# Reordering the opening transfers of a Fourier-mixing and ELU-MLP kernel: x first, then the filter in two halves, with the weight conversions spread anew

## The chip, the cores and the metric

The kernel runs on one core of one Trainium2 chip. The metric is device time in microseconds (us), the time of the slowest core, and here there is only one. Its engines are named as in the profile: PE is the matrix engine TensorE, PEld its weight loads, DVE is VectorE, ACT is ScalarE, POOL is GpSimd, SP is SyncE. "Landed" means that a transfer's completion was seen by whoever waited for it.

## The reference

Eight sequences of 3008 rows by 256 channels are filtered in the frequency domain, and every row then goes through an MLP with an ELU between its two matrices.

```python
batch, seq, dim = (8, 3008, 256)
X = np.fft.rfft(x, axis=1)
F = (filt_r + 1j * filt_i)[None, :, :]           # 1505 frequencies x 256
y = np.fft.irfft(X * F, n=x.shape[1], axis=1)
h = y.reshape(24064, 256) @ w_in                 # 256 x 2048
g = np.where(h > 0.0, h, np.exp(np.minimum(h, 0.0)) - 1.0)
out = g @ w_out                                  # 2048 x 256
```

## The kernel before

The transform of one sequence is split in stages, and between stages the data are turned round through DRAM. For the first sequence these stages run alone; those of the other seven run inside the MLP's work. The MLP is 192 "quads" of matmuls. The opening, which the change touches, has these parts:

- `x_load`: six chunks of x (two transfers of 256 KB each on the SyncE queue) and six tables `ta` (ScalarE queue). Only four chunk buffers exist.
- `a_unit`: four matmuls per chunk on TensorE, evicted by ScalarE (L168). `z_write` puts the result in DRAM, `z_read` brings it back in another order.
- `f_read_first`: the filter, 22 transfers on the GpSimd queue into one large buffer `ff`. Half `a = 0` lies on partitions 0 to 47, half `a = 1` on 64 to 110; `c` is 0 for the real part and 1 for the imaginary part.
- the filter loop: eight `b_unit`s. Each has four VectorE products with `ff` (L223 to L226), two GpSimd combinations, then inverse matmuls, and a write to DRAM (`y_write`).
- `w_fetch(k)`, `w_convert(k)`: 16 blocks of weights (512 KB each) are fetched on the GpSimd queue into three rotating buffers and turned from 64-bit to 32-bit numbers by VectorE and ScalarE. The odd blocks have four adds more.
- `y_read`, `n_unit`: the last stage (psn, L266), whose output the first quad needs.

```python
    def f_read_first(t):
        for c, src in enumerate((filt_r, filt_i)):
            for a in range(2):
                r = a * 64
                nc.gpsimd.dma_start(t[r:r + 24, :, c, :, :].rearrange("q g u d -> q g (u d)"),
                                    raw(src, 2 * a, [[64 * D, 24], [4 * D, NG], [1, 2 * D]]))
                for u in range(2):
                    g0 = 1 if a == u == 0 else 0
                    for r0, n in ((24, 16), (40, 7)):
                        nc.gpsimd.dma_start(t[r + r0:r + r0 + n, g0:NG, c, u, :], ...)   # cut: source rows
            nc.gpsimd.dma_start(t[24:48, 0, c, 0, :], raw(src, 32, [[64 * D, 24], [1, D]]))
# ... cut ...
            for k in range(2):
                w_fetch(k)
            for c in range(XBUFS):
                x_load(0, c, nc.scalar)
            nc.vector.memset(ff, 0.0)
            nc.gpsimd.tensor_copy(out=junk[0:1], in_=xs[0, 2][0:1, 0, 0:1])
            # ... cut: small tables ...
            w_fetch(2)
            f_read_first(ff)
            for c in range(NXC):
                a_unit(0, c)
                if c + XBUFS < NXC:
                    x_load(0, c + XBUFS, nc.scalar)
                z_write(0, c)
                w_convert(c)
                w_fetch(3 + c)
            z_read(0, 0)
            z_read(0, 1)
            for g in range(NG + 2):
                # ... cut: bi_unit(g - 2), b_unit(g), z_read(g + 2), y_write(g - 2) ...
                if g % 2 == 1:
                    k = 6 + g // 2
                    w_convert(k)
                    w_fetch(k + 3)
```

In the trace of this kernel ScalarE waits 21.16 us for a weight block while an eviction whose matmuls ended by 25 us stands behind it (the line is in the prediction); and GpSimd issues that block at 46.98 us, behind all 22 transfers of the filter (18.63 to 46.44 us).

Of the kernel before, what the change touches and what calls it, by code (L numbers as in the profile page):

```python
# [26 lines left out]
D = 256  # L27
# [5 lines left out]
NXC = H // XC  # L33
NG = K2 // 4
XBUFS = 4
# [60 lines left out]
def kernel(  # L96
# [9 lines left out]
    nc = tc.nc  # L106
# [37 lines left out]
    def raw(src, row, ap):  # L144
        return bass.AP(tensor=src.tensor, offset=src.offset + row * D, ap=ap)
# [15 lines left out]
    def a_unit(b, c):  # L161
        t = t1s[b, c] = t1p.tile([P, XC, D], FP32, tag="t1", name="t1")
        xt, w = xs.pop((b, c)), tas.pop((b, c))
        for r in (0, 2):
            ps = psM.tile([P, 2, D], FP32, tag="mx", name="psa")
            for u in range(2):
                nc.tensor.matmul(ps[:, u, :], w[:, r + u, :], xt[:, r + u, :], start=True, stop=True)  # L167
            nc.scalar.activation(out=t[:, r:r + 2, :], in_=ps, func=AXT.Copy)  # L168
# [19 lines left out]
        for a, r in enumerate((LO, HI)):  # L188
            nc.gpsimd.dma_start(t[r].rearrange("p c u d -> p (c u d)"), fd[g, a].rearrange("q c u d -> q (c u d)"))

    def f_read_first(t):


        for c, src in enumerate((filt_r, filt_i)):
            for a in range(2):
                r = a * 64
                nc.gpsimd.dma_start(t[r:r + 24, :, c, :, :].rearrange("q g u d -> q g (u d)"),
                                    raw(src, 2 * a, [[64 * D, 24], [4 * D, NG], [1, 2 * D]]))
                for u in range(2):
                    g0 = 1 if a == u == 0 else 0  # L200
                    for r0, n in ((24, 16), (40, 7)):
                        nc.gpsimd.dma_start(t[r + r0:r + r0 + n, g0:NG, c, u, :],
                                            raw(src, 64 * (r0 - 23) - 4 * g0 - 2 * a - u,
                                                [[64 * D, n], [-4 * D, NG - g0], [1, D]]))
            nc.gpsimd.dma_start(t[24:48, 0, c, 0, :], raw(src, 32, [[64 * D, 24], [1, D]]))



# [304 lines left out]
    with tc.manual_schedule():  # L513


        with tc.tile_pool(name="boot", bufs=1) as bp:
            ff = bp.tile([P, NG, 2, 2, D], FP32, name="ff")
            for k in range(2):
                w_fetch(k)
            for c in range(XBUFS):  # L520
                x_load(0, c, nc.scalar)
            nc.vector.memset(ff, 0.0)
            nc.gpsimd.tensor_copy(out=junk[0:1], in_=xs[0, 2][0:1, 0, 0:1])
            for t, d in ((gb, gb_d), (gr, gr_d), (gi, gi_d)):
                nc.gpsimd.dma_start(t, d)
            w_fetch(2)
            f_read_first(ff)
            for c in range(NXC):
                a_unit(0, c)
                if c + XBUFS < NXC:  # L530
                    x_load(0, c + XBUFS, nc.scalar)
                z_write(0, c)
                w_convert(c)
                w_fetch(3 + c)
            z_read(0, 0)
            z_read(0, 1)
            for g in range(NG + 2):
                if g >= 2:
                    bi_unit(0, g - 2)
                if g < NG:  # L540
                    b_unit(0, g, ff[:, g])
                    if g + 2 < NG:
                        z_read(0, g + 2)
                if g >= 2:
                    y_write(0, g - 2)
                if g % 2 == 1:
                    k = 6 + g // 2
                    w_convert(k)
                    w_fetch(k + 3)
        yp = pool("yp", 2)  # L550
        gp = pool("gp", 2)
        ep = pool("ep", 2)
        op = pool("op", 1)
        y_read(0, 0)
        w_convert(11)
        w_fetch(14)
        nc.scalar.dma_start(eye, id_d)
        n_unit(0, 0)
        x_load(1, 0)



        PER = 24
        plan = {}

        def at(quad, place, fn, *a):
            plan.setdefault((quad, place), []).append((fn, a))

        for c in range(1, XBUFS):
            at(c - 1, 0, x_load, 1, c)  # L570
        for k in range(12, 16):
            at((0, 0, 1, 2)[k - 12], 1, w_convert, k)
        at(0, 1, w_fetch, 15)
        at(3, 1, f_arrange)
        for f in fbufs:
            at(4, 1, nc.vector.memset, f, 0.0)
        for b in range(B):
            t = (b - 1) * PER
            if b > 0:
                for c, s in enumerate((0, 2, 3, 4, 6, 7)):  # L580
                    at(t + s, 0, a_unit, b, c)
                    nb, nxt = (b, c + XBUFS) if c + XBUFS < NXC else (b + 1, c + XBUFS - NXC)
                    if nb < B:
                        at(t + s, 0, x_load, nb, nxt)
                    at(t + s, 0, z_write, b, c)
                for g in range(NG + 2):
                    s = t + 9 + g
                    if g >= 2:
                        at(s, 1, bi_unit, b, g - 2)
                    if g < NG:  # L590
                        at(s, 1, b_unit, b, g)
                    if g >= 2:
                        at(s, 1, y_write, b, g - 2)
                for g in range(NG):
                    s = t + 7 + g
                    at(s, 1, f_read, b, g)
                    at(s, 1, z_read, b, g)
            for m, (s, place) in enumerate(((20, 0), (25, 1), (29, 1), (32, 0), (36, 0), (40, 0))):
                if b > 0 or m > 0:
                    at(t + s - (1 if m == 0 else 2), 0, y_read, b, m)  # L600
                    at(t + s, place, n_unit, b, m)
                at(t + PER + 4 * m + 5, 0, o_unit, b, m)

        items = [(b, m, q) for b in range(B) for m in range(6) for q in range(4)]
        for i in range(-PER, len(items) + 2):
            ups, up_tail = up_steps(*items[i]) if 0 <= i < len(items) else ((), None)
            downs, down_tail = down_steps(*items[i - 1]) if 1 <= i <= len(items) else ((), None)
            ups, downs = list(ups), list(downs)
            for k in "UDUDUDUUD":
                s = ups if k == "U" else downs  # L610
                if s:
                    s.pop(0)()
            for fn, a in plan.get((i, 0), ()):
                fn(*a)
            for k in "UDUDD":
                s = ups if k == "U" else downs
                if s:
                    s.pop(0)()
            if up_tail:
                up_tail()  # L620
            if down_tail:
                down_tail()
            for fn, a in plan.get((i, 1), ()):
                fn(*a)
# [32 lines left out]
```

## Time and profile before

| | before |
|---|---|
| median of 4 runs | 2763.99 us (2762.85 to 2765.96) |
| profiled span | 2761.7 us |
| last eviction of x (ACT L168) starts | 61.02 us |
| last z write landed / z read back | 68.3 / 73.7 us |
| filter: first issue / last landed | 18.6 / 53.4 us |
| second product step (DVE L224) starts | 75.40 us |
| last product of the loop ends | 115.55 us |
| psn starts | 131.14 us |

I use the second product step, not the first, as the mark where the loop runs: the first needs only the filter's real part, the second needs the imaginary part too. Before, the two are 0.6 us apart.

These are stretches of the kernel before, from the view that sums each engine's busy time in a window. Where stretches are shown, the columns are the window, its length, the busy time of each engine with its number of instructions, TensorE's granted clock as a share of full speed (PEclk), the share of the 16 DMA engines that was busy, and GB/s.

```profile
core 0: us, PE busy (x) PEld busy (x) DVE busy (x) ACT busy (x) POOL busy (x), PEclk, DMA share, GB/s
50.00:73.70 23.70, 2.86 (x11) 1.45 (x14) 13.86 (x29) 6.40 (x11) 3.91 (x7) 0.50 0.76 219
0.00:73.70 73.70, 19.04 (x59) 12.46 (x62) 33.12 (x55) 15.48 (x26) 22.61 (x44) 0.70 0.94 225
...
74.79:115.55 40.76, 28.16 (x115) 8.92 (x108) 36.59 (x58) 9.78 (x18) 21.18 (x20) 0.63 0.57 156
```

### The profile page before, as it was taken

To read this page: it belongs to the slowest core of one execution; us is meant where nothing else is said; L and a number is where in the kernel's file an instruction comes from. 1 tells how busy PE (TensorE), PEld (TensorE's weight loads), DVE (VectorE), ACT (ScalarE), POOL (GpSimd) and SP (SyncE) were. 2 spreads that over 40 slices of the span, in tenths; PEclk is the share of its full clock that TensorE was granted. 3 is DMA by queue.
4 is the path that set the end of the run, shared out by engine and by line. 5 is a ranking of instruction groups with operands and counts; after the bars stand their busy time and mean duration, and the time that the engine had idled before them with its cause. 6 is when DMAs were issued, how large, how long until landed. Compare 5 with 4: busy or idle time off the path is not lost.

```text
span 2761.7 us, 36465 instructions
## 1 busy us (share of the span) xinstructions
PE 2661.4 (96%) x13376; PEld 2281.0 (83%) x13376; DVE 2021.7 (73%) x3428; ACT 1331.3 (48%) x2281; POOL 268.4 (10%) x322
## 2 busy tenths in 40 slices
PE   2689999999999999999999999999999999999998
PEld 1288778987899878998789877898789987899887
DVE  4777877777776777767776787767877677777776
ACT  2254455544455444554455544454454544454544
POOL 3311210002000120001200021000210012000000
PEclk7599999999999999999999999999999999999999
DMA  9654421433114331242313332143321223110100
GB/s 227 174 136 119 106 56 30 115 90 99 43 47 117 76 91 37 70 115 71 79 50 87 87 88 68 37 106 94 97 61 39 72 69 94 37 39 19 25 22 16
DMA packets 141634, 214.51 MB, mean 78 GB/s; under 512 B 25268, under 2 KB 99142, under 8 KB 141456
## 3 DMA queue, kind: packets, MB, share of 16 engines
q1 hardware_dynamic: 122656, 173.60, 24.7%
q0 software_dynamic: 17792, 36.93, 5.4%
q8 instruction: 106, 1.74, 0.3%
q10 hardware_dynamic: 1008, 1.64, 0.2%
q14 instruction: 72, 0.59, 0.1%
HBM read 137.04 MB, written 78.12 MB: 78 GB/s over the span
## 4 chain that ended last, share of the span: by engine, by line
PE 86%; DVE 7%; ACT 3%; DMA 2%; issue 2%; POOL 0%; SPq 0%; DVEq 0%; ACTq 0%; POOLq 0%
PE po L385 37%; PE pha L312 11%; PE phc L312 11%; PE phd L312 11%; PE phb L312 5%; PE psa L167 3%; PE psn L266 2%; PE pva L211 2%; PE psr L211 2%; PE pso L424 2%; DVE g L317 1%; ACT e L323 1%; ACT e L324 1%; DVE c L403 1%; DVE g L328 1%
## 5 line engine op out<-in xcount | busy, mean ns | idle before, releaser
L385 PE MATMUL po<-g,wo 128*128 128x256 f32 (+1 forms) x5376 | 1324.2, 375 | 0.0
L385 PEld LDWEIGHTS po<-g,wo 128*128 128x128 f32 x5376 | 1021.5, 190 | 116.2
L323 ACT ACTIVATE e<-g 128x512 f32<-128x512 f32 (+1 forms) x576 | 357.6, 621 | 599.5 <-DVE g L317 599.3
L324 ACT ACTIVATE e<-e 128x512 f32<-128x512 f32 (+1 forms) x768 | 477.6, 622 | 24.4
L312 PE MATMUL pha<-y,wi 128*128 128x256 f32 (+1 forms) x1536 | 396.3, 380 | 8.7 <-ACT g L332 8.6
L317 DVE TENSOR_TENSOR g<-phc,g 128x512 f32<-128x512 f32 (+1 forms) x384 | 259.5, 676 | 194.9 <-PE phc L312 194.8
L328 DVE SCALAR_TENSOR_TENSOR g<-e,g 128x512 f32<-128x512 f32 (+1 forms) x576 | 387.4, 673 | 11.6 <-ACT e L324 11.1
L323 ACT ACTIVATE e<-pha 128x512 f32<-128x512 f32 (+1 forms) x192 | 113.0, 588 | 531.1 <-PE pha L312 531.1
L312 PEld LDWEIGHTS pha<-y,wi 128*128 128x128 f32 x1536 | 285.2, 190 | 93.1 <-ACT t L238 34.1
L317 DVE TENSOR_TENSOR g<-phd,g 128x512 f32<-128x512 f32 (+1 forms) x384 | 261.0, 680 | 87.0 <-PE phd L312 66.0
L328 DVE SCALAR_TENSOR_TENSOR g<-e,pha 128x512 f32<-128x512 f32 (+1 forms) x192 | 129.4, 674 | 257.8 <-ACT e L324 257.8
L227 POOL TENSOR_TENSOR sr<-sr,sp 128x512 f32<-128x512 f32 x64 | 81.1, 1268 | 1304.4 <-DVE sp L225 1304.4
L312 PE MATMUL phc<-ys,wi 128*128 128x256 f32 (+1 forms) x768 | 195.5, 377 | 2.6 <-DVE si L224 2.6
L312 PE MATMUL phd<-y,wi 128*128 128x256 f32 (+1 forms) x768 | 195.4, 377 | 1.3
L312 PE MATMUL phb<-ys,wi 128*128 128x256 f32 (+1 forms) x768 | 193.8, 375 | 0.4 <-DVE ys L290 0.4
L312 PE MATMUL phc<-y,wi 128*128 128x256 f32 (+1 forms) x768 | 194.0, 375 | 0.0
L312 PE MATMUL phd<-ys,wi 128*128 128x256 f32 (+1 forms) x768 | 193.7, 375 | 0.0
L312 PEld LDWEIGHTS phc<-ys,wi 128*128 128x128 f32 x768 | 145.3, 191 | 23.7 <-issue 7.8
L312 PEld LDWEIGHTS phd<-y,wi 128*128 128x128 f32 x768 | 145.3, 191 | 22.5 <-PE phc L312 6.5
L332 ACT ACTIVATE g<-pha 128x512 f32<-128x512 f32 (+1 forms) x192 | 112.7, 587 | 105.3 <-PE pha L312 105.1
L312 PEld LDWEIGHTS phb<-ys,wi 128*128 128x128 f32 x768 | 145.8, 190 | 17.2 <-PE pha L312 0.7
L312 PEld LDWEIGHTS phd<-ys,wi 128*128 128x128 f32 x768 | 145.8, 190 | 16.5
(98 smaller groups left out, 2781.1 us busy)
## 6 DMA issues: line engine op xcount, KB each, us to landing
z<-t SPq DMA_DIRECT2D x192, 128.0 KB, 3.8
t<-z SPq DMA_DIRECT2D x128, 192.0 KB, 3.7
yd<-t SPq DMA_DIRECT2D x128, 192.0 KB, 2.8
t<-yd SPq DMA_DIRECT2D x192, 128.0 KB, 4.1
xc<-in_x_dram SPq DMA_DIRECT2D x88, 256.0 KB, 4.6
out_dram<-o SPq DMA_DIRECT2D x176, 128.0 KB, 2.4
f<-fd POOLq DMA_DIRECT2D x112, 192.0 KB, 3.6
tn<-tn_t SPq DMA_DIRECT2D x48, 256.0 KB, 4.2
```

The lines of the kernel that those rows point to most:

```text
L167: nc.tensor.matmul(ps[:, u, :], w[:, r + u, :], xt[:, r + u, :], start=True, stop=True)
L211: nc.tensor.matmul(ps[:, u:u + w, :], table[k, v, :], rhs[k, u:u + w, :], start=True, stop=True)
L227: nc.gpsimd.tensor_tensor(out=sr, in0=sr, in1=p, op=ALU.subtract)
L266: nc.tensor.matmul(ps[:, ts(q, P)], t[:, i - 4 * m, ds(dh * P, P)], w[:, i - 4 * m, :], start=True, stop=True)
L312: nc.tensor.matmul(banks[key][:, a, 0:h], w_in[q][:, COMBO[n], a, :], y[n], start=start and a == 0, stop=True, skip_group_check=True)
L317: nc.vector.tensor_tensor(out=g[o], in0=i0, in1=i1, op=ALU.add)
L323: nc.scalar.activation(out=e, in_=src, func=AXT.Relu, scale=-1.0)
L324: nc.scalar.activation(out=e, in_=e, func=AXT.Exp, scale=-1.0)
L328: nc.vector.scalar_tensor_tensor(out=g[n], in0=es[n], scalar=1.0, in1=src, op0=ALU.subtract, op1=ALU.max)
L332: nc.scalar.activation(out=g["t1"], in_=mm(1, "a", True), func=AXT.Copy)
L385: nc.tensor.matmul(po[i][:, u, 0:h], w_out[q][:, COMBO[n], a, :], g[n][:, a, :], start=q == 0 and a == 0 and n in (1, 3, 6, 4), stop=True, ...
L424: nc.tensor.transpose(ps[0:w, u, ts(dh, P)], c[dh][:, ds((2 * a + u) * P, w)], eye)
```

## The change

Its intent: nothing that the first products don't need should stand before x, so that x, z and the z read are done early; the filter follows, half by half; conversions fill the waits, so that fewer are left for the MLP.

```diff
-    def f_read_first(t):
+    def f_read_first(t, a):
+        r = a * 64
         for c, src in enumerate((filt_r, filt_i)):
-            for a in range(2):
-                r = a * 64
             ... (one main and four mirrored transfers per c, as before)
-            nc.gpsimd.dma_start(t[24:48, 0, c, 0, :], ...)
+            if a == 0:
+                nc.gpsimd.dma_start(t[24:48, 0, c, 0, :], ...)
...
+        CONVERTS = {0: 6, 1: 7, 3: 8, 5: 9, 7: 10, 8: 11}
+            def after(c):
+                nc.gpsimd.tensor_copy(out=junk[0:1], in_=xs[0, c][0:1, 0, 0:1])
-            nc.vector.memset(ff, 0.0)
-            nc.gpsimd.tensor_copy(out=junk[0:1], in_=xs[0, 2][0:1, 0, 0:1])
+            nc.gpsimd.memset(ff, 0.0)
+            w_convert(0)
...
             w_fetch(2)
-            f_read_first(ff)
+            w_fetch(3)
             for c in range(NXC):
+                if c + XBUFS < NXC + 2 and c >= 2:
+                    x_load(0, c + XBUFS - 2, nc.scalar)
+                if c == NXC - 1:
+                    after(NXC - 1)
                 a_unit(0, c)
-                if c + XBUFS < NXC:
-                    x_load(0, c + XBUFS, nc.scalar)
                 z_write(0, c)
-                w_convert(c)
-                w_fetch(3 + c)
+                if c == 1:
+                    w_convert(1)
+            f_read_first(ff, 0)
+            w_convert(2)
+            w_fetch(4)
+            w_fetch(5)
+            f_read_first(ff, 1)
             z_read(0, 0)
             z_read(0, 1)
+            for k in range(3, 6):
+                w_convert(k)
+                w_fetch(k + 3)
...
-                if g % 2 == 1:
-                    k = 6 + g // 2
+                if g in CONVERTS:
+                    k = CONVERTS[g]
                     w_convert(k)
                     w_fetch(k + 3)
...
-        w_convert(11)
-        w_fetch(14)
+        for k in (12, 13):
+            w_convert(k)
+            if k == 12:
+                w_fetch(15)
...
-        for k in range(12, 16):
-            at((0, 0, 1, 2)[k - 12], 1, w_convert, k)
-        at(0, 1, w_fetch, 15)
+        for k in (14, 15):
+            at(k - 14, 1, w_convert, k)
```

More of the change, by code (lines that the diff above doesn't have):

```diff
@@ L189, in f_read @@
             nc.gpsimd.dma_start(t[r].rearrange("p c u d -> p (c u d)"), fd[g, a].rearrange("q c u d -> q (c u d)"))
-    def f_read_first(t):
+    def f_read_first(t, a):
+        r = a * 64
         for c, src in enumerate((filt_r, filt_i)):
-            for a in range(2):
-                r = a * 64
-                nc.gpsimd.dma_start(t[r:r + 24, :, c, :, :].rearrange("q g u d -> q g (u d)"),
-                                    raw(src, 2 * a, [[64 * D, 24], [4 * D, NG], [1, 2 * D]]))
-                for u in range(2):
-                    g0 = 1 if a == u == 0 else 0
-                    for r0, n in ((24, 16), (40, 7)):
-                        nc.gpsimd.dma_start(t[r + r0:r + r0 + n, g0:NG, c, u, :],
-                                            raw(src, 64 * (r0 - 23) - 4 * g0 - 2 * a - u,
-                                                [[64 * D, n], [-4 * D, NG - g0], [1, D]]))
-            nc.gpsimd.dma_start(t[24:48, 0, c, 0, :], raw(src, 32, [[64 * D, 24], [1, D]]))
+            nc.gpsimd.dma_start(t[r:r + 24, :, c, :, :].rearrange("q g u d -> q g (u d)"),
+                                raw(src, 2 * a, [[64 * D, 24], [4 * D, NG], [1, 2 * D]]))
+            for u in range(2):
+                g0 = 1 if a == u == 0 else 0
+                for r0, n in ((24, 16), (40, 7)):
+                    nc.gpsimd.dma_start(t[r + r0:r + r0 + n, g0:NG, c, u, :],
+                                        raw(src, 64 * (r0 - 23) - 4 * g0 - 2 * a - u,
+                                            [[64 * D, n], [-4 * D, NG - g0], [1, D]]))
+            if a == 0:
+                nc.gpsimd.dma_start(t[24:48, 0, c, 0, :], raw(src, 32, [[64 * D, 24], [1, D]]))
     def tile_mm(ps, table, k, rhs, special):
```

## The prediction

> **What bounds the kernel now.** I read the page first, then the chain of waits over the first 180 us, then the same stretch in order of time and by stage. On the page TensorE is 96% busy and the chain that ended last is 86% TensorE, so outside the opening almost nothing is to be had; the kernel is 192 FFN quads after a start. The change touches only that start: the first 185 us or so of 2761.7. The stretches of it:
>
> ```profile
> core 0: us, PE busy (x) PEld busy (x) DVE busy (x) ACT busy (x) POOL busy (x), PEclk, DMA share, GB/s
> 20.00:30.00 10.00, 3.79 (x16) 2.71 (x16) 5.13 (x12) 1.20 (x2) 3.65 (x7) 0.98 1.10 253
> 30.00:40.00 10.00, 0.00 (x0) 0.00 (x0) 1.45 (x3) 1.09 (x2) 4.37 (x8) 0.50 1.06 201
> ...
> 50.00:60.00 10.00, 0.00 (x0) 0.00 (x0) 5.10 (x11) 2.82 (x5) 2.14 (x4) 0.50 0.79 228
> ...
> 90.00:100.00 10.00, 6.25 (x30) 2.10 (x23) 9.37 (x16) 3.28 (x6) 4.25 (x5) 0.67 0.60 179
> ```
>
> Until 50 us the transfers are the limit (share over 1, 200 to 250 GB/s) and every compute engine is idle half the time or more. From 75 to 115 us (the filter loop, eight units) VectorE is the limit: 9.4 of 10 us here, of which the weight conversions are nearly half. The chain says which transfers:
>
> ```profile
> 20.04 13.04 DMA ff<-in_filt_r_dram
> 33.08 0.28 issue
> 33.36 0.55 POOL ff L205
> 33.90 11.16 DMA ff<-in_filt_i_dram
> ...
> 47.58 6.99 DMA f<-in_moe_w_out_dram
> ...
> 63.43 4.87 DMA z<-t
> 68.36 4.28 DMA t<-z
> ...
> 120.92 3.78 DMA yd<-t
> ...
> 126.00 5.00 DMA t<-yd
> ```
>
> First the filter (all its 22 transfers go out on the GpSimd queue between 18.6 and 47.0 us), then the weight block of conversion 3, queued behind the filter, only then the last z write and read back. Why a weight block can hold x is seen in the order of time on ScalarE:
>
> ```profile
> 32.43 1.09 ACT L168 ACTIVATE t<-psa 128x512 f32<-128x512 f32 x2 [3.48 <-DMA z<-t]
> ...
> 54.67 0.67 ACT L471 ACTIVATE wl<-f 128x512 f32<-128x512 uint32 x1 [21.16 <-DMA f<-in_moe_w_out_dram]
> ...
> 55.77 1.06 ACT L168 ACTIVATE t<-psa 128x512 f32<-128x512 f32 x2
> ...
> 61.02 1.07 ACT L168 ACTIVATE t<-psa 128x512 f32<-128x512 f32 x2
> ```
>
> ScalarE works in program order. Conversion 3 stands ahead of the eviction of x chunk 4, so that eviction waits 21.16 us for a weight block, though its matmuls ended by 25 us; chunk 5's eviction comes at 61.02 for the same reason. The first filter product (VectorE) starts at 74.79, the last product ends at 115.55, the FFN's first matmuls (psn) at 131.14. One more place, behind the first FFN quad:
>
> ```profile
> 153.31 1.86 PE L312 MATMUL pha<-y,wi 128*128 128x224 f32 x4 [7.05 <-ACT g L332]
> ```
>
> Conversions 12 and 13 run together there (VectorE 148.09 to 157.1), TensorE is idle 7.05 us, and its granted clock falls to a half for some 10 us.
>
> [...] z writes issued from 20 to 40 us, beside the filter, took about 16 us to land, against 3.8 us in the median of the whole kernel. So holding the filter back really speeds x and z; it doesn't remove bytes. [...] the first two conversion steps take 0.43 us alone, 0.88 and 1.49 us when the GpSimd add of a filter unit runs. [...] VectorE's clearing of ff takes 6.88 us, so I estimate GpSimd's at 6 to 9 us. No long GpSimd clear is in the trace to test that.
>
> **The change, part by part.**
>
> *Clearing ff* moves to GpSimd: VectorE is free 6.88 us sooner, GpSimd sits in it from about 2.6 to 10 us. Before, GpSimd then waited until 15.77 for x chunk 2, so the small tables and weight block 2 go out some 5 us earlier than they did, and block 3 soon after. Some 1.2 MB now meets x chunks 2 and 3 (at 230 GB/s up to 5 us of sharing, perhaps 2 us of delay).
>
> *x first.* Chunks 4 and 5 now come after z writes 0 and 1 in the SyncE queue, but nothing of the filter goes out until chunk 5 has landed. In the trace z writes 0 went out at 15.9; I put z 1 at 19 to 20, chunk 4 out at about 23 and chunk 5 at about 28, landed at 34 to 35 (7 us, the landing time of x issued from 10 to 20 us). No weight stands ahead of the evictions that could be late (conversions 0 and 1 only), so the last eviction is at about 37 instead of 62.1. That is 25 us off the first chain, but it is not the gain.
>
> *Filter.* Half 0 (12 transfers, 1.5 MB) goes out from 35, beside the z writes 3 to 5; at 0.6 us an issue and with waits for earlier landings about 10 us. Then blocks 4 and 5 (the latter waits for conversion 2, whose ScalarE part stands behind the last eviction: done at about 41), then half 1 from about 46. Blocks and half are 2.5 MB, at 230 to 260 GB/s 10 to 11 us: landed at about 57 to 58. The z read back is earlier: last z landed at about 46, read by 51. Cross-check by bytes: x 3.1, ta 1.6, z 3.1, filter 3.0, six weight blocks 3.0, z read 0.8, tables 0.2: 14.8 MB, at 250 GB/s 59 us.
>
> *Conversions 3 to 5* now stand before the first filter unit. From this trace a conversion is 3.74 us of VectorE alone (60.03 to 63.77), 5.46 with the four combining adds (54.66 to 60.12). Conversion 5 can start when block 5 has landed and 4 is done, about 54, and ends at about 60. So first filter product at about 61 (transfers and VectorE nearly tie) instead of 74.79: **14 us gained**, give or take 6.
>
> *Filter loop.* Before, conversions 6, 7 and 8 stood ahead of the last product; now 6, 7, 8 and 9. Beside GpSimd one with adds takes 6.98 us (90.24 to 97.22). VectorE was busy 36.6 of the 40.8 us, so about 1.5 us of idle absorbs some: **5.5 us lost**. Then 10 and 11 instead of 9 and 10 in the ScalarE order before the last eviction: **about 1 lost**. Conversions 12 and 13 fill the 10 us in which yd is written and read (VectorE needs 10 plus 11, 12, 13 there, about 20 us from the last product; psn's eviction came 17.7 after it): at most 1 to 2 us over, **1 lost**.
>
> *FFN.* One conversion (14) after quad 0, one (15, with adds) after quad 1, none after quad 2, in place of two, one, one. After quad 0 5.4 us of VectorE and ScalarE waiting go, and the gap shrinks to about 2[...]: 10 groups at half clock from 153.31 on cost up to 3 us. After quad 1 1.7 us more VectorE work. **7 gained.**
>
> Sum: 14 - 5.5 - 1 - 1 + 7 = 13.5, and I round to 14: 2764 - 14 = **2750 us**.
>
> **Rivals.** (a) *Half 1 of the filter takes the place of the weight wait, and later than I think*: it is queued behind block 5 and so behind all of A's evictions; if its transfers take 25 us as two halves did before (18.6 to 54), the first product is at 70 and the gain is 5: 2759. For it: z writes and weight blocks still share. Against: the old filter shared with x, ta and z together. (b) *The loop takes nothing and the transfers run well*: first product at 56, conversion 9 mostly in idle time, clock kept in the FFN: gain 25, 2739. For it: weights issued after 50 us landed in 4.5 us. Against: VectorE idle in the loop is only 4.2 us. (c) *x comes later*: chunks 4 and 5 behind two z writes on SyncE, and ScalarE stalls in its own issue of ta 4 and 5 ahead of evictions; if chunk 5 lands at 45, all that follows is 10 later: 2760. (d) *No gain at all*, the bytes being the same: the DMA share of 0.79 from 50 to 70 speaks against it: there was room, and nobody to ask for it.
>
> **Range and chances.** The sum's worst likely combination is 0 to 3 gained, the best 27: 2737 to 2763. 2% is 55 us, nearly the whole stretch before the first filter product, and no part offers it; a loss of 55 would take a new stall as long as the whole filter.
>
> **What would show it.** The last x eviction at 35 to 40 us with no wait on a weight; filter transfers none before about 33; the first product of the filter at 58 to 64, ended by conversion 5 or the filter; last product 45 to 47 us after the first (40.8 now); no 7 us gap after quad 0 and no fall of the clock there. I am wrong if chunk 5 lands after 42, if half 1 lands after 65, or if the loop stretches by over 9 us.

## The result, and the profile after

Ratios in this document are the mean time of one kernel's fast runs over that of the other's of the same rounds, so they are not quite the ratio of the medians quoted beside them; a 95% interval stands in brackets.

| | runs | median us | lowest to highest | ratio to before |
|---|---|---|---|---|
| before | 4 | 2763.99 | 2762.85 to 2765.96 | |
| after | 4 | 2767.73 | 2762.17 to 2770.96 | 1.0011 [0.9993, 1.0028] |

By the 2% mark that is the same time. It is not the 2750 us that I predicted, and it lies outside my range of 2737 to 2763. The four runs of the kernel after are spread over 8.8 us, those of before over 3.1 us; that spread will matter. The profile fell on the slowest of the four, 2770.96 us, so the pieces below are those of a slow execution.

| us | before | after | difference |
|---|---|---|---|
| last eviction of x starts | 61.02 | 36.68 | -24.3 |
| x chunk 5 landed | 41.1 | 34.5 | -6.6 |
| last z write landed | 68.3 | 51.0 | -17.3 |
| z read back | 73.7 | 67.0 | -6.7 |
| filter, last landed | 53.4 | 76.0 | +22.6 |
| second product step | 75.40 | 76.00 | +0.60 |
| last product ends | 115.55 | 125.44 | +9.89 |
| psn starts | 131.14 | 144.21 | +13.07 |
| span | 2761.7 | 2769.2 | +7.5 |

The differences of the last four rows, taken piece by piece, are +0.60 up to the second step, +9.29 in the loop (40.15 to 49.44 us), +3.18 from the loop to psn (15.59 to 18.77), and -5.57 from psn to the end (2630.56 to 2624.99). They add up to +7.5.

The chain of waits of the kernel after (start, length, what):

```profile
34.35 7.46 DMA ff<-in_filt_r_dram
...
42.10 9.09 DMA ff<-in_filt_i_dram
...
51.47 15.36 DMA ff<-in_filt_r_dram
...
68.02 10.52 DMA f<-in_moe_w_out_dram
```

Compare it with the chain of before: x, z and the weight blocks among them have gone, and the chain runs through nothing but the filter from 34 to 67 us, then through weight block 6, fetched on the same queue behind it. That x really comes first is one line on ScalarE, the last eviction:

```profile
36.68 0.60 ACT L168 ACTIVATE t<-psa 128x512 f32<-128x512 f32 x1 [0.22 <-PE psa L167]
```

In brackets is the wait: 0.22 us for the matmul, and no weight block. The GpSimd queue of the kernel after shows where the second half stood:

```profile
49.59 0.68 POOL L196 DMA_DIRECT2D ff<-in_filt_r_dram  x1 [3.11 <-DMA ff<-in_filt_i_dram]
...
65.16 0.57 POOL L201 DMA_DIRECT2D ff<-in_filt_i_dram  x1 [1.32 <-DMA ff<-in_filt_r_dram]
```

The first transfer of half 1 went out at 49.59 us, the last at 65.16, although an issue costs only some 0.6 us (0.68 and 0.57 in these two lines): ahead of seven of the ten issues GpSimd waited 0.30 to 3.69 us, 13.4 us together, for earlier transfers of the filter or a weight block to land. So slow transfers delayed the issue of the next. And the transfers were slow:

```profile
core 0: us, PE busy (x) PEld busy (x) DVE busy (x) ACT busy (x) POOL busy (x), PEclk, DMA share, GB/s
45.35:75.97 30.62, 7.83 (x20) 2.13 (x20) 9.51 (x19) 2.40 (x4) 9.79 (x17) 0.50 1.04 168
...
50.00:60.00 10.00, 1.93 (x4) 0.73 (x4) 4.37 (x9) 1.92 (x4) 4.26 (x8) 0.50 1.04 182
60.00:70.00 10.00, 5.90 (x16) 1.40 (x16) 5.14 (x10) 0.49 (x1) 2.92 (x6) 0.50 1.07 137
...
76.00:125.44 49.44, 31.75 (x108) 8.63 (x108) 42.67 (x68) 11.71 (x21) 21.80 (x21) 0.50 0.52 145
...
0.00:76.00 76.00, 25.05 (x68) 14.23 (x68) 27.61 (x56) 15.29 (x25) 29.49 (x45) 0.74 0.99 215
```

The first line runs from the issue of weight block 4 to the landing of half 1: 30.62 us at 168 GB/s are 5.1 MB, of which blocks 4 and 5 and half 1 are 2.6 MB. The rest is z: the last z writes (landed by 51.0) and the z reads of the first four units (issued from 46.2 on), with the end of half 0 and, from 67.4 on, the first of weight blocks 6 to 8. In the two windows from 50 to 70 us the DMA share is over 1, so the engines were taken all the time, yet they moved 182 and then only 137 GB/s. Over the whole opening it is 215 GB/s for 76 us, 16.3 MB: about what before moved by 73.7 us. The fourth line is the loop: VectorE is busy for 42.67 us in place of 35.98 from the second step on. Where those went is in its order of time:

```profile
76.00 0.69 DVE L224 TENSOR_TENSOR si<-psr,ff 128x512 f32<-128x512 f32 x1 [6.51 <-DMA ff<-in_filt_i_dram]
...
111.24 1.12 DVE L470 TENSOR_SCALAR wm<-f 128x512 uint32<-128x512 uint32 x1
...
118.38 0.68 DVE L223 TENSOR_TENSOR sr<-psr,ff 128x512 f32<-128x512 f32 x1
...
122.96 0.69 DVE L223 TENSOR_TENSOR sr<-psr,ff 128x512 f32<-128x512 f32 x1 [2.11 <-PE psi L211]
```

The first line is the second product step: it waits for the imaginary part of the filter. The second and third are the beginning and the end of conversion 9, which stood behind the last product before: 118.38 - 111.24 = 7.14 us. The fourth is a wait of 2.11 us for TensorE. Before, the loop had two such waits, of 1.04 and 2.11 us; after it has three, of 1.04, 2.11 and 2.11. So 7.14 + 2.11 = 9.25, nearly the 9.29 us. (Summed over the whole loop, VectorE's busy time grew by 6.69 us and its idle time by 2.60, in which a wait of 0.76 us for weight block 6 is new too.) TensorE's granted clock in the loop is 0.50 in place of 0.63, which goes with that third wait; what lowers it I have not tested.

What the change did win, behind the first quad of the MLP, on TensorE:

```profile
163.10 1.86 PE L312 MATMUL pha<-y,wi 128*128 128x224 f32 x4 [3.40 <-ACT g L332]
```

The gap is 3.40 us where it was 7.05.

### The profile page after: what moved, and what is told of

Same layout as the page of the kernel before. It is cut to its first block, busy times and chain, and to the rows that moved or that the text cites. A ratio compares the mean times of both kernels' runs of the same rounds, so it can differ in the third digit from the quotient of the medians.

```text
span 2769.2 us, 36476 instructions
## 1 busy us (share of the span) xinstructions
PE 2668.7 (96%) x13376; PEld 2280.8 (82%) x13376; DVE 2018.0 (73%) x3427; ACT 1332.5 (48%) x2281; POOL 275.9 (10%) x323
## 4 chain that ended last, share of the span: by engine, by line
PE 86%; DVE 7%; ACT 3%; issue 2%; DMA 2%; POOL 0%; DVEq 0%; SPq 0%; ACTq 0%; POOLq 0%
PE po L385 37%; PE pha L312 11%; PE phc L312 11%; PE phd L312 11%; PE phb L312 5%; PE psa L167 3%; PE psn L266 2%; PE pva L211 2%; PE psr L211 2%; PE pso L424 2%; DVE g L317 1%; ACT e L323 1%; ACT e L324 1%; DMA ff<-in_filt_r_dram 1%; DVE c L403 1%
## 5 line engine op out<-in xcount | busy, mean ns | idle before, releaser
L312 PEld LDWEIGHTS phc<-ys,wi 128*128 128x128 f32 x768 | 144.8, 190 | 23.7 <-issue 7.8
```

The costliest lines, as they stand in the source:

```text
L312: nc.tensor.matmul(banks[key][:, a, 0:h], w_in[q][:, COMBO[n], a, :], y[n], start=start and a == 0, stop=True, skip_group_check=True)
```

## The experiments

All kernels of one call ran on one chip and share the runs of the kernel before. "Opening" is the time of the second product step in the profiled run. Where an expectation names a theory by a letter, H is the theory that the order by half is at fault (a half lies on one side of the partitions), and O that holding the filter behind x is.

| run | median us (runs) | before, same call | ratio | opening us | span us |
|---|---|---|---|---|---|
| after_again | 2768.70 (5) | 2762.88 | 1.0019 [1.0005, 1.0033] | 75.86 | 2767.1 |
| by_part | 2764.85 (5) | 2762.88 | 1.0008 [0.9995, 1.0020] | 70.76 | 2763.1 |
| blocks_last | 2773.54 (4) | 2762.88 | 1.0038 [1.0024, 1.0052] | 81.88 | 2773.8 |
| before_halves | 2763.95 (4) | 2762.88 | 1.0005 [0.9991, 1.0019] | 75.06 | 2761.9 |
| source_straight (wrong result) | 2762.06 (1) | 2762.71 | | 69.69 | 2760.3 |
| both_sides (wrong result) | 2764.83 (1) | 2762.71 | | 68.90 | 2763.1 |
| one_side | 2769.84 (1) | 2762.71 | | 75.23 | 2768.1 |
| old_converts | 2762.25 (5) | 2762.71 | 0.9998 [0.9984, 1.0011] | 69.72 | 2757.9 |
| alternate | 2762.05 (5) | 2762.57 | 0.9995 [0.9982, 1.0007] | 69.36 | 2760.3 |
| filter_early | 2770.25 (5) | 2762.57 | 1.0026 [1.0013, 1.0040] | 76.96 | 2770.0 |
| filter_early_old | 2767.40 (5) | 2762.57 | 1.0019 [1.0007, 1.0032] | 78.26 | 2768.1 |
| alone | 2919.61 (1) | 2762.57 | | | 2917.8 |
| alternate_old | 2758.31 (5) | 2762.69 | 0.9984 [0.9970, 0.9997] | 68.66 | 2757.5 |
| two_queues | 2760.85 (5) | 2762.69 | 0.9995 [0.9982, 1.0007] | 73.57 | 2759.6 |

### after_again: the kernel after, once more

No edit; it shows how far the result repeats.

> The changed kernel once more, as the yardstick of this call. All theories: 2762 to 2771 us, the filter's second half issued from about 49.6 us and landed at about 76, first filter product complete in its four steps only then. If the second half lands here by 65, the 26 us of the first profile were an accident of that execution and the case is another.

Measured: 2768.70 us, ratio 1.0019 [1.0005, 1.0033]. The second half went out at 50.2 and landed at 75.8 us. The result repeats, and the kernel after is slower by about 0.2%, a difference that is real and far below the 2% mark.

### by_part: the filter by component instead of by half

Both halves of the real part are issued first, then, at the place of the second half, both halves of the imaginary part.

```diff
-    def f_read_first(t, a):
-        r = a * 64
-        for c, src in enumerate((filt_r, filt_i)):
+    def f_read_first(t, c):
+        src = (filt_r, filt_i)[c]
+        for a in range(2):
+            r = a * 64
```

> The changed kernel, with the 22 filter transfers split between the two places by component (all real ones first, 11, then all imaginary ones, 11), not by half of the partitions; bytes, weights and places in the queue are otherwise the same. Theory H (a lone half is slow: all its transfers go to partitions 64 to 111 and read one half of each 4 KB): the second batch takes about 13 us, lands at about 62 to 64, the first filter product is at about 65 in place of 75 and the time falls by about 10, to 2757. Theory W (the second batch is late because two weight blocks stand before it and its last issues wait for their landing): as the changed kernel, landed at about 74 to 76, 2766. Theory B (the same bytes, so the same end): as W.

Measured: the second batch went out at 48.6 and landed at 70.7 us, 22.1 us where the half took 26.4, and the opening is 5.2 us earlier than in the kernel after. The time is 2764.85. In the mean of five runs each, it is 3.2 us faster than after_again (2765.13 against 2768.36). So the order of the same transfers matters, by some 3 us; the 5 us of the two profiles are less sure, because an opening of one order varies as much (see old_converts). And 70.7 is far from the 58 that I had predicted: the order by half is not the whole cause.

### blocks_last: weight blocks 4 and 5 behind the second half

```diff
             w_convert(2)
+            f_read_first(ff, 1)
             w_fetch(4)
             w_fetch(5)
-            f_read_first(ff, 1)
```

> The changed kernel with weight blocks 4 and 5 fetched after the filter's second half. Theory H: the half still goes slowly once alone, 18 to 20 us, but starts about 4 us earlier and shares less: landed at about 65 to 68; blocks 4 and 5 land at about 70, conversion 5 ends at about 76, so the first product is no earlier, 2765 to 2770. Theory W: the half lands at 57 to 60, then blocks 4 and 5 at 64, first product at about 70, 2761. The landing of the half tells them apart, more than the time.

Measured: the second half went out at 46.0 and landed at 69.5 us, so it still took 23.4 us with no block ahead of it. Blocks 4 and 5 went out at 58.2 and 60.2 and landed at 72.2 and 75.8; conversions 4 and 5 stand ahead of the first product, which then came at 81.28. This is the slowest order, 2773.54 us. Blocks in front of the filter are not most of what makes it slow; and here what goes last is late.

### before_halves: the kernel before with the filter by half

```diff
-            f_read_first(ff)
+            f_read_first(ff, 0)
+            f_read_first(ff, 1)
```

> The kernel before with nothing changed but the order of its filter transfers: all of half 0, then all of half 1. Theory H: the second half slower, filter landed at about 60 in place of 54, block 3 behind it later, so the last eviction of x and the first filter product 5 to 8 us later: 2769 to 2772. Theories W and B: no change, 2763 to 2765.

Measured: filter from 18.3 to 52.9 us, in place of 18.6 to 53.4; 2763.95 us, ratio 1.0005. In the old place the order by half costs nothing that these runs show. There x, tables and z move beside it; in the new place weight blocks and z reads do. An order can be free in one company and cost some 3 us in another; why, no run shows.

### source_straight: the same partitions, from contiguous rows (wrong)

The mirrored part of the filter is read backwards, in rows that lie far apart. Here the sources are contiguous ascending rows and the destinations are unchanged. The result is wrong (relative error 0.50).

```diff
-                                raw(src, 2 * a, [[64 * D, 24], [4 * D, NG], [1, 2 * D]]))
+                                raw(src, 384 * a, [[16 * D, 24], [2 * D, NG], [1, 2 * D]]))
 ... (the mirrored sources likewise)
```

> Wrong result on purpose. The changed kernel, its 22 filter transfers in the same order to the same places in SBUF with the same bytes, but each reads rows that lie one behind the other in DRAM, ascending, not rows 64 KB apart and descending. Theory S (the slow second half is the scattered source): half 1 takes 12 to 15 us instead of 26, the first product is complete at 63 to 66 instead of 76. Theory D (it is where they write: 48 of 128 partitions): no change, 75 to 77.

Measured: second half from 46.9 to 69.7 us, 22.8 us; opening 69.69. Alone this looks as if the scattered source cost 6 us. The run old_converts below forbids that reading: it has the opening of the kernel after to the letter, scattered sources included, and its opening came at 69.72.

### one_side and both_sides: which partitions the second batch goes to

Both issue the second batch component by component in turn. one_side puts all of it on partitions 64 to 110, as the change does (correct). both_sides puts the imaginary part on partitions 0 to 47 instead (wrong, relative error 0.31). Bytes, sources and the number of transfers are equal.

```diff
+            for c in range(2):
+                main(c, 64)                    # one_side
+                main(c, 64 * (1 - c))          # both_sides
 ... (the mirrored transfers likewise, c innermost)
```

> The yardstick of both_sides: the same order of the transfers of half 1 (real and imaginary alternating), all to partitions 64 to 110 as they should be; result correct. All theories: as the changed kernel, first product complete at 75 to 77, 137 to 180 GB/s from 50 to 70 us.

> Wrong result on purpose. The changed kernel; the second batch reads exactly what half 1 reads, but its real part goes to partitions 64 to 110 and its imaginary part to 0 to 46, alternating. Theory D: about half the time in the second batch, 13 to 17 us, first product at 64 to 68, and over 190 GB/s from 60 us on where the changed kernel had 137. Theory S: no faster than the run one_side, first product at 75 to 77.

Measured: one_side landed from 49.1 to 75.2 us (26.1 us), both_sides from 48.6 to 68.9 (20.3 us). The window of 60 to 70 us in one_side:

```profile
core 0: us, PE busy (x) PEld busy (x) DVE busy (x) ACT busy (x) POOL busy (x), PEclk, DMA share, GB/s
60.00:70.00 10.00, 5.24 (x17) 1.39 (x16) 2.52 (x6) 0.00 (x0) 1.16 (x2) 0.50 1.00 135
```

The same window in both_sides:

```profile
core 0: us, PE busy (x) PEld busy (x) DVE busy (x) ACT busy (x) POOL busy (x), PEclk, DMA share, GB/s
60.00:70.00 10.00, 6.86 (x19) 1.62 (x17) 3.03 (x7) 0.00 (x0) 3.33 (x6) 0.50 0.94 201
```

201 against 135 GB/s, at no higher DMA share. Each is a single run, and the spread told under old_converts is as large; the run alone repeats it with nothing beside it.

### alone: the same batches by themselves

Where the filter's first half went out, nine batches are read into `ff` first (one of half 0, then two rounds of four on the place of half 1), each followed by a GpSimd copy that waits until it has landed. The filter is then cleared and read as usual, so the result is correct, and the kernel is longer by the probes.

```diff
+            for _ in range(2):
+                for side, straight in (("one", False), ("both", False), ("one", True), ("both", True)):
+                    probe(ff, 1, side, straight)      # 10 transfers, 1.5 MB
+                    landed()                          # GpSimd copies from ff
+            nc.gpsimd.memset(ff, 0.0)
```

> A measurement by itself, result correct, time of no interest (some 120 us longer). The changed kernel with ten batches of filter transfers put in after the last x chunk, each waiting for the one before to land: a first with half 0, then twice four batches with the bytes of half 1 (1.5 MB): to partitions 64 to 110 (one), real part there and imaginary part to 0 to 46 (both), each with the scattered source of the kernel and with a straight one. Nothing else is under way but the z writes at the very start. Floor from issuing: 10 issues at 0.6 us and a landing, 8 to 9 us. Theory D (destination): one 11 to 14 us with either source, both 8 to 10. Theory S (source): scattered 11 to 14 with either destination, straight 8 to 10. Theory X (the half is slow only because it runs against weight blocks and z reads): all four 8 to 10 us.

Measured, from the first issue to the start of the copy that waited for the landing, in us:

| | one side | both sides |
|---|---|---|
| scattered source, first round | 23.7 (z reads beside it) | 12.5 |
| scattered source, second round | 16.9 | 12.1 |
| straight source, first round | 17.1 | 13.7 |
| straight source, second round | 16.6 | 14.6 |

The second round's scattered batches, first the one-sided, then the one on both sides:

```profile
core 0: us, PE busy (x) PEld busy (x) DVE busy (x) ACT busy (x) POOL busy (x), PEclk, DMA share, GB/s
121.90:138.80 16.90, 0.00 (x0) 0.00 (x0) 0.00 (x0) 0.00 (x0) 5.73 (x11) 0.50 0.76 91
...
139.30:151.40 12.10, 0.00 (x0) 0.00 (x0) 0.00 (x0) 0.00 (x0) 5.71 (x10) 0.50 0.68 127
```

With every compute engine but GpSimd idle, the same 1.5 MB take 16.9 us into one side and 12.1 into both. Every time is longer than the theory of the destination had expected (11 to 14 and 8 to 10), but they stand to one another as it had them. The source makes no such difference: 16.9 against 16.6 into one side, and into both the straight source is even slower by 1 to 2.5 us, which stays unexplained. So the destination side matters, and the scattered source is not what is slow. It is one execution with two rounds. By what mechanism the side matters, no run shows.

But even both sides alone move only 127 GB/s; my estimate assumed 230 to 260. In this trace eight transfers of a batch go out in some 4.5 to 5 us, and in all nine batches the ninth waits for an earlier one to land, 0.45 to 5.82 us: in these batches no more than eight were under way on the GpSimd queue, and so slow transfers at the head held the tail back.

### old_converts: the new opening, the old conversions from the loop on

```diff
-        CONVERTS = {0: 6, 1: 7, 3: 8, 5: 9, 7: 10, 8: 11}
+        CONVERTS = {1: 6, 3: 7, 5: 8, 7: 9, 9: 10}
 ...
-        for k in (12, 13):
-            w_convert(k)
-            if k == 12:
-                w_fetch(15)
+        w_convert(11)
+        w_fetch(14)
 ...
-        for k in (14, 15):
-            at(k - 14, 1, w_convert, k)
+        for k in range(12, 16):
+            at((0, 0, 1, 2)[k - 12], 1, w_convert, k)
+        at(0, 1, w_fetch, 15)
```

> The changed kernel's opening with the conversions of the filter loop and of the FFN placed as in the kernel before (6 to 10 after units 1, 3, 5, 7 and 9, 11 behind the loop, 12 and 13 after quad 0, 14 after quad 1, 15 after quad 2). If conversion placement in the loop costs what the profiles show: last product 41 us after the first complete one (50 in the changed kernel), FFN start at about 132 (144), then the FFN loses 5 to 6 again; 2767 minus 12 plus 6, 2761 to 2763. If the loop was long for another reason (TensorE at half clock all through it), the loop stays at 47 to 50 us and the time is 2770 or more.

Measured: 2762.25 us, ratio 0.9998 [0.9984, 1.0011]: about 6 us under the medians of the kernel after. From its second step to its last product are 42.22 us (after 49.44, before 40.15), from there to psn 16.01 (after 18.77, before 15.59), and psn to end 2630.0 (after 2625.0, before 2630.6). Two lines of it in order of time, the second product step and the matmul behind quad 0:

```profile
69.72 0.69 DVE L224 TENSOR_TENSOR si<-psr,ff 128x512 f32<-128x512 f32 x1 [3.61 <-DMA ff<-in_filt_i_dram]
...
150.60 1.86 PE L312 MATMUL pha<-y,wi 128*128 128x224 f32 x4 [7.06 <-ACT g L332]
```

The 7.06 us gap is back, and with it the 5 us that the MLP had gained; but 7.2 us of the loop and 2.8 before psn have gone. So the conversions moved forward cost 10 us to win 5. What is left of the loop's excess over before, 2.07 us, is the third wait of 2.11 us for TensorE, which is here too, at a clock of 0.58. It does not come from the conversions, which stand as before. But it does not come with every new opening either: in two_queues, below, the loop takes 40.08 us at a clock of 0.63, as it did before (40.15 at 0.63).

The first line holds the other finding. Up to the loop this program is that of the kernel after, and yet its opening is at 69.72, not at 76.00 and 75.86. The profile fell on the fastest of its five runs (2759.71). The three profiles of one and the same opening land its filter at 69.7, 75.8 and 76.0 us, and that is the likely reason why the four runs of the kernel after are spread over 8.8 us. The chip or the call alone do not explain it: one_side, of the same call as old_converts, had its opening at 75.23. So a difference of 6 us between two openings, each seen once, shows nothing.

### alternate: the filter by component, with the sides in turn

As by_part, with main and mirrored transfers going to the two sides alternately.

```diff
+        for a in range(2):
+            ... main transfer of side a
+        for r0, n in ((24, 16), (40, 7)):
             for u in range(2):
-                g0 = 1 if a == u == 0 else 0
-                for r0, n in ((24, 16), (40, 7)):
+                for a in range(2):
+                    ... mirrored transfer of side a
```

> The run by_part once more (real part, blocks 4 and 5, imaginary part) with the transfers to partitions 0 to 47 and 64 to 110 alternating inside each part, so that at any time about half the bytes under way go to either side; result correct. Theory D: second batch landed at 63 to 67, first product complete at 64 to 68, 2757 to 2761. Theory S or X: as by_part, 71, 2765.

Measured: filter landed at 69.3 us, opening 69.36; 2762.05 us, some 6 us under the kernel after and level with before (0.9995 [0.9982, 1.0007]). Five runs lie between 2758.82 and 2764.58. Its opening is 6.6 us earlier than the slow openings of the order by half (76.00, 75.86) and hardly earlier than the fast one (69.72); so in the mean over executions it wins, and it does not bring the filter to 58 either.

### filter_early and filter_early_old: is x first worth anything?

The whole filter goes out right behind weight block 3, in the order of before, with no wait for x; all else of the change stays. filter_early_old has the old conversions as well.

```diff
             w_fetch(3)
+            f_read_first(ff)
             for c in range(NXC):
 ...
-                if c == NXC - 1:
-                    after(NXC - 1)
 ...
-            f_read_first(ff, 0)
             w_convert(2)
             w_fetch(4)
             w_fetch(5)
-            f_read_first(ff, 1)
```

> The changed kernel without its holding back: the whole filter, in the order of the kernel before, goes out right after weight block 3 and no longer waits for x; blocks 4 and 5 after it; evictions of x are still ahead of all conversions but 0 and 1. Theory O (what held the kernel before was the order of weight conversions against evictions on ScalarE, and the overlap of filter with x and z is worth having): x evicted at about 43, filter landed at about 55, first product complete at 60 to 63, 50 us of loop as in the changed kernel, FFN start at about 130, 2755 to 2758. Theory R (x first is what is worth having): x evicted at 50 or later, first product at 68 or later, no better than the changed kernel.

> filter_early with the later conversions placed as in the kernel before (run old_converts). Theory O: first product at 60 to 63, loop 41 us, FFN start at about 120, and 5 to 6 lost again after it: 2750 to 2754, faster than both kernels. Theory R: 2762 to 2766.

Measured: 2770.25 and 2767.40 us, both slower than before. The filter landed at 54.7, but x chunk 5 only at 55.0 and the z read at 72.0; the opening is at 76.96. ScalarE's evictions in filter_early:

```profile
34.12 1.08 ACT L168 ACTIVATE t<-psa 128x512 f32<-128x512 f32 x2 [13.66 <-DMA z<-t]
...
57.28 0.60 ACT L168 ACTIVATE t<-psa 128x512 f32<-128x512 f32 x1 [9.53 <-DMA z<-t]
```

The first eviction waits 13.66 us for a z write, which must land before its buffer is free, and those writes run beside the filter. (In the kernel before, the nine z writes issued from 20 to 40 us, beside the filter, took 15.8 us to land in the median; in the kernel after, with none of the filter under way, the 16 issued from 14 to 34 us took 3.7.) The second wait, 9.53 us, is put down to a z write as well, but most of it is for x: chunk 5 landed only at 55.02 and its matmuls began at 55.15. So holding the filter behind x is right, given the rest of this opening: without it the kernel is slower by about 5 us with the old conversions (2767.40 against 2762.25, and the fastest run of the first is slower than the slowest of the second). With the new conversions it is about 2 us (2770.25 against the 2767.73 and 2768.70 of after), which is within their spread. These are medians of different calls whose before agree within 0.3 us, but for the 2767.73, whose before was 1.4 higher. It moved 219 GB/s up to 73 us, 16.0 MB: again about the same bytes by the same time.

### alternate_old: the new opening with alternating sides, and the old conversions

As alternate, with the edit of old_converts. It joins what seemed good.

> Both repairs in one: the filter transfers alternating between the partition sides by part (run alternate) and the later conversions placed as in the kernel before (run old_converts). If the two causes are separate, their savings add: 2768 minus 6 (alternate) minus 6 (old_converts), 2754 to 2758, FFN start at 128 to 131 minus nothing, faster than both kernels by 0.2 to 0.3%. If both removed the same delay (the filter only has to be earlier than something else), 2760 to 2763. In the profile the first complete product at 66 to 70 and a loop of 41 to 42 us.

Measured: 2758.31 us (2756.51 to 2759.33), ratio 0.9984 [0.9970, 0.9997]. It is the fastest kernel here and beats both, before by 4.4 us and after by about 10; against old_converts, which differs in the filter's order alone, it is 3.9 us faster. Against before that is 0.16% of the time, well within the 2% band. In its profile:

```profile
core 0: us, PE busy (x) PEld busy (x) DVE busy (x) ACT busy (x) POOL busy (x), PEclk, DMA share, GB/s
0.00:68.60 68.60, 25.43 (x68) 14.37 (x68) 28.50 (x55) 15.59 (x25) 29.30 (x45) 0.68 0.98 234
```

234 GB/s over the opening in place of 215, 16.1 MB by 68.6 us, with a share of 0.98: the opening is full. But it is not full of needed bytes alone. By the sizes of the issues, what the loop's first two units wait for (x, its tables, z written and read, the filter, six weight blocks) is 15.0 MB; the rest, about 1 MB, is z reads of later units and weight blocks 6 to 8, which no run held back. The time is just above the expected 2754 to 2758, and opening and loop (42.22 us) are as expected. Against before in pieces: -6.74 to the second step, +2.07 in the loop, +1.12 to psn, -0.65 to the end, together -4.2, which is the difference of the spans (2757.5 and 2761.7).

### two_queues: the imaginary part on the SyncE queue

```diff
-            f_read_first(ff, 0)
+            f_read_first(ff, 0, nc.gpsimd)
+            f_read_first(ff, 1, nc.sync)
             w_convert(2)
             w_fetch(4)
             w_fetch(5)
-            f_read_first(ff, 1)
```

(against alternate_old)

> alternate_old with the imaginary part of the filter issued on the SyncE queue behind the z writes, beside the real part on GpSimd; blocks 4 and 5 then follow the real part at once. If the rest of the filter's slowness is issuing (0.6 us each on one queue and at most eight under way there), the filter lands at 58 to 61, the first product comes at 60 to 63, and the time is 2748 to 2753. If the rest is bytes and partitions (the DMA engines are busy all of the time), it lands at 65 to 69 and the time is as alternate_old or worse, z being read later.

Measured: 2760.85 us, ratio 0.9995, opening 73.57: no better than one queue. Now the z reads stand behind the filter's transfers in SyncE's queue; these are their issues on it:

```profile
60.89 0.31 SPq L183 DMA_DIRECT2D t<-z  x1
...
64.02 0.30 SPq L184 DMA_DIRECT2D t<-z  x1
```

In alternate_old the z read had already landed at 60.9 us. What one queue has gained, the other has lost. The loop takes 40.08 us, without the third wait for TensorE.

## Why the prediction was wrong

It held a change of 2% (55 us) to be out of reach, which came true, and it named a time of 2750 us, which did not. Two of its own three signs of being wrong came: half 1 landed after 65, and the loop stretched by over 9 us. Point by point, by its own steps:

- **Clearing ff on GpSimd**: predicted 6 to 9 us, an estimate from VectorE's 6.88 us in the kernel before; measured 6.93. Right.
- **x first**: last eviction predicted at about 37 with no wait on a weight; 36.68 to 37.28. Right, and chunk 5 landed at 34.5 as predicted. So rival (c) is out. The last z write was predicted at 46 and landed at 51.0; the z read back was predicted at 51 and came at 67.0, while filter transfers were under way beside it (the z reads issued from 45 to 77 us took 10.7 us to land in the median, those of before from 50 to 75 us 4.3).
- **Filter half 1**: this is the step that failed. The prediction put it: "Blocks and half are 2.5 MB, at 230 to 260 GB/s 10 to 11 us: landed at about 57 to 58." Half 1 went out at 49.6, not 46, and took 26.4 us. Both factors were wrong. The bytes: from the issue of block 4 to the landing of half 1 the engines moved 5.1 MB, of which blocks and half are 2.6, since z and then blocks 6 to 8 went along. The rate: they moved 168 GB/s, not 230 to 260, at a share of 1.04. The rate was taken from stretches with other traffic, and put on a batch of filter transfers which, even alone, moves 91 GB/s into one side and 127 into both. An estimate from the run alone: of the 26.4 us, 16.9 would be there with nothing beside it, 5 of them for going to one side; the rest, about 10, is sharing. Block 5 landed at 59.2 instead of 54, so conversion 5 was done at 64.7 instead of 60. The first product was due at 61; the second step, which needs the whole filter, came at 76. The term "14 us gained" measured -0.6 in the profiled run of after, and +5.7 in the same opening's best execution.
- **The cross-check by bytes** failed too: "14.8 MB, at 250 GB/s 59 us". Its count of the needed bytes was right to 0.2 MB. But by the last needed landing the opening moves 16.0 to 16.6 MB, in the orders looked at (before, after, filter_early, alternate_old), at 215 to 234 GB/s: 69 to 76 us. The kernel before had the DMA engines 94% busy until then. With all these bytes its room was about the 5.7 us worked out above, not 14, and the best order won 6.7 in the opening. Whether more can be won by holding back the 1 to 1.6 MB that are not yet needed (estimated at 234 GB/s, 4 to 7 us) was not tried.
- **Filter loop**: predicted +5.5, measured +9.3. Conversion 9 cost its whole 7.14 us, none of it hidden, because VectorE's idle time lies at other places (waits for TensorE); 2.11 us more come from a third such wait, which stays when the old conversions are put back (old_converts).
- **To psn**: predicted +2 in two pieces, measured +3.2.
- **MLP**: predicted -7, measured -5.6. The gap behind quad 0 shrank to 3.40 us, not 2, and the clock fell there even so (0.83 of full in 160 to 170 us of the kernel after). That it would keep its full value behind a gap of 2 us was my guess, which no run here tests. The prediction counted 10 groups of matmuls at half clock before; the chain shows four of them slow (1.86 to 1.34 us each in place of 0.76), and two after.
- **The rivals**: (a) named what happened, the filter's half taking the place of the weight wait and needing 25 us; but I gave it a gain of 5 us, since I let half 1 go out at 45 and the other terms stand. (d), no gain because the bytes are the same, was set aside with "there was room, and nobody to ask for it". There was room for about 6 us with the same bytes, and (d) was nearer the truth than the prediction.

With its own last terms as measured (+9.3, +3.2, -5.6: a loss of 6.9), the change could have reached 2750 only with 21 us won in the opening. It won none in the slow executions and some 6 in the fast ones, so by this sum it ends between 1 and 7.5 us behind.

What is shown by runs: the conversions moved into the loop and before psn cost more than the MLP gives back (old_converts); the new place of the filter is right (filter_early_old against old_converts); the side of the partitions makes a lone batch slow, 16.9 us against 12.1, its scattered source does not, 16.9 against 16.6 (alone); in the old place the order by half costs nothing (before_halves). What stays open: how much of the late landing is owed to each of the transfers beside the filter, and so what an opening without blocks 6 to 8 and the later z reads would win; why one opening lands its filter at 69.7 in one execution and 76.0 in another; and what keeps TensorE's clock lower in the loop. So the step that failed is sure and measured; its cause is shown in part.

## What to carry to other kernels

Before you count what a new order of transfers wins, multiply out how much idle transfer time there is up to the last landing that is needed: as long as the same bytes move by then at the same rate, the order can win little more than that (here 5.7 us of room, 6.7 won). So count also the bytes that move by then without being needed: they are the other thing to win. Take a transfer rate from a stretch that moves the same kind of transfer (here a lone filter batch moved 91 to 127 GB/s, the opening as a whole 215 to 234); and let consecutive transfers in a queue go to different sides of the partitions, if the trace shows a difference as it does here. Work moved from one idle gap into another is free only if the engine is idle at that very place, not on average (here conversion 9 cost the loop its whole 7.14 us).
